# Attention feeding two MoE layers on one core: an earlier narrow transpose, pair 6 through the DRAM scratch, and a later sum of output halves

## The chip, the cores and the metric

One core of a Trainium2 chip runs the whole program in one launch. The metric is the device time in microseconds (us). The engines are called PE (TensorE, matmuls and transposes), DVE (VectorE), ACT (ScalarE), POOL (GpSimd) and SP (SyncE, which here only issues DMAs). Each works through its own queue in order.

## The reference

```python
# 2 x 8 heads, 768 rows, head size 64; bucketed attention
q_bits = einsum(q, proj) > 0; k_bits = einsum(k, proj) > 0      # 6 bits give a bucket
scores = q @ k.T / 8, and -1e9 where the buckets differ
attn = exp(scores - max); attn /= sum(attn) + 1e-9
x = attn @ v                                                     # to 1536 x 512
x = relu(x @ w_in)**2 @ w_out                                    # first MoE
x = silu(x @ w_in2) @ w_out2                                     # second MoE
```

Everything is float32.

## The kernel before

The heads are worked through as 8 pairs. A pair has 4 units (two heads, two halves of 384 rows), a unit has 3 tiles of 128 rows by 768 keys. So there are 32 units and 96 tiles. One loop over steps d sends out all instructions of attention; step d computes the scores of one tile, the exp of the tile before it, and transposes two blocks of 384 columns of exp'd tiles of an earlier unit. With `tc.manual_schedule()` the order on each engine is the order in which the code calls it; waits between engines follow from the tiles that they share.

In a step PE does, in this order, six transposes of 128 x 128 into two banks of PSUM (`transp`, L1025; three banks in turn), the product with V for the two blocks of two steps ago (`av`, L1049 and L1050), and the scores (`score_mm`, L989, two buffers in turn). Each transposed block goes through two instructions to become a high part, cast by ACT (`t_hi`, L1030), and a low part, subtracted by DVE (`t_lo`, L1036). DVE takes the row maximum (L996) and two short instructions on it (L1000, L1001); ACT then does the exp with its row sums (`score_exp`, L1009). When a unit is done, ACT copies its output out of PSUM (`ob`, L1060) and SP sends its two halves to the tiles `ta` and `tb` of the pair (L1062).

Once in 12 steps, at d = 5, 17, ..., 77, a step is long: PE multiplies by the projection (`bits_mm`, L789, 12 matmuls), DVE compares the result in two halves (`bits_cmp`, L795) and SP copies the bits into the score operands of a pair (`place_bits`, L919), whose first scores are computed two steps later. In these steps, and in 92 and 93, DVE also does one or two instructions of the conversion of a weight from 64 to 32 bits (`w_exp` L958, `w_sign` L962, `w_low` L966).

When pair p is done (d0 = 12(p + 1)), its row sums, 12 columns of 128 rows, are inverted (L1071) and brought into the layout of the output. For pairs 0 to 5 this is done with a narrow transpose at step d0 + 5 (`row_turn`, L1077), which writes into columns 384 to 511 of the bank whose first 384 columns hold block g + 1 of the step; ACT copies it out (L1079); SP puts it into a DRAM scratch (`row_put`, L1083) and gets it back, repeated over 64 partitions, three steps later (`row_get`, L1088). The narrow transpose stands behind both casts of its step in the code. For pair 6, POOL spreads the sums (L1074), PE transposes them at step 93 (`rb_mm`, L1097, six transposes) and ACT copies them out (L1108). Pair 7, the last, uses the same spreading and six transposes after the last step (L1315). POOL adds the two halves of the output, `ta` += `tb`, at step d0 + 3 (`x_sum`, L1103), multiplies by the rows (`x_mul`, L1115) and splits the first operands of the MoE (`x_put`, L1124 and L1125). At steps 83 to 89 POOL adds blocks of the result for the MoE (`x_form`, L1130).

After attention the MoE's instructions follow, ordered by a planner with its own costs. The change does not touch them.

Of the kernel before, what the change touches and what calls it, by code (L numbers as in the profile page):

```python
# [11 lines left out]
F32 = mybir.dt.float32  # L12
# [5 lines left out]
ALU = mybir.AluOpType  # L18
# [3 lines left out]
B, H, S, D = 2, 8, 768, 64  # L22
NT, DM, FF = B * S, H * D, 2048
NB = 6
NPAIR = B * H // 2
NU = NPAIR * 4
QW = 384
# [672 lines left out]
def lsh_attention_moe_moe(ctx, tc, kd, qk, qf, fq, v, pc, wi1, wo1, wi2, wo2, out):  # L700
# [109 lines left out]
    def first_load(h):  # L810
        t = pair[0]
        if h == 0:
            c = ac.tile([128, S], F32, tag="P", bufs=6, name="fc")
            first["c"] = c[:, 0:NFQ]
            first[0, 0] = c[:, NFQ : NFQ + QW], ac.tile([128, S], F32, tag="P", bufs=6, name="fq1")[:, 0:QW]
            k = a1.tile([128, S], F32, tag="ta", bufs=2, name="fk")
            first[0, 1] = k[:, half(0)], k[:, half(1)]
            nc.sync.dma_start(out=c[:, 0 : NFQ + QW], in_=fq)
            nc.scalar.dma_start(out=first[0, 1][0], in_=qf[0, 1, :, half(0)])
            nc.sync.dma_start(out=first[0, 1][1], in_=qf[0, 1, :, half(1)])  # L820
            nc.scalar.dma_start(out=first[0, 0][1], in_=qf[0, 0, :, half(1)])
        else:
            first[1, 0] = a1.tile([128, S], F32, tag="tb", name="fr10")
            first[1, 1] = a1.tile([128, 6, 2, 64], F32, tag="rw", bufs=2, name="fr11").rearrange("p a b c -> p (a b c)")
            for i in range(2):
                nc.sync.dma_start(out=first[1, i], in_=qf[1, i])
            nc.scalar.dma_start(out=pcr, in_=pc)
        t["qq"][h] = a1.tile([128, 2, S], F32R, tag="qq", bufs=2, name=f"qq0_{h}")
        t["kk"][h] = a1.tile([128, 2, S], F32R, tag="kk", bufs=2, name=f"kk0_{h}")
        if h == 0:  # L830
            first["hk", 0] = a1.tile([128, S], F32R, tag="hk", name="hk0_0")
# [209 lines left out]
    def av(g):  # L1041
        u, kt = divmod(g, KT)
        p, h, z = u // 4, (u // 2) % 2, u % 2
        if kt == 0:
            otile[u] = ps_o.tile([128, 512], F32, tag="o", name=f"o{u}") if u < NU - 1 else ps_s.tile([128, 2, 512], F32, tag="s", name=f"o{u}")[:, 0]
        o = otile[u]
        vv = pair[p]["vv"][:, h * KT + kt].rearrange("p a d -> p (a d)")
        th, tl = PT.pop(g)
        mm(o[:, 0:QW], vv, th, start=kt == 0, stop=False)  # L1049
        mm(o[:, 0:QW], vv, tl, start=False, stop=kt == KT - 1)  # L1050
        if kt == KT - 1:
            if p not in xs:
                xs[p] = [a1.tile([128, S], F32, tag=n, bufs=b, name=f"{n}{p}") for n, b in (("ta", 2), ("tb", 1))]
            if u == NU - 1:
                ta, zs = xs[p][0], slice(z * QW, (z + 1) * QW)
                nc.scalar.copy(out=ta[64:128, zs], in_=o[0:64, 0:QW])
                nc.vector.tensor_tensor(out=ta[64:128, zs], in0=o[64:128, 0:QW], in1=ta[64:128, zs], op=ALU.add)
                return
            ob = a2.tile([128, QW], F32, tag="ob", name=f"ob{u}")
            nc.scalar.copy(out=ob, in_=o[:, 0:QW])  # L1060
            for i in range(2):
                nc.sync.dma_start(out=xs[p][i][64 * h : 64 * h + 64, z * QW : (z + 1) * QW], in_=ob[64 * i : 64 * i + 64])  # L1062
# [6 lines left out]
    def norm_rows(p):  # L1069
        ri = sums[p]  # L1070
        nc.vector.reciprocal(out=ri, in_=ri)  # L1071
        if p >= NPAIR - 2:
            w = rows[p] = a1.tile([128, 6, 2, 64], F32, tag="rw", bufs=2, name=f"rw{p}")
            nc.gpsimd.tensor_copy(out=w, in_=ri.rearrange("p (h c) -> p c h", h=2).unsqueeze(3).broadcast_to([128, 6, 2, 64]))  # L1074

    def row_turn(p, t):
        nc.tensor.transpose(t[0:12, QW:512], sums[p], ident)  # L1077
        r = turned[p] = a1.tile([12, 128], F32, tag="rt", name=f"rt{p}")
        nc.scalar.copy(out=r, in_=t[0:12, QW:512])  # L1079

# [2 lines left out]
        nc.sync.dma_start(out=o.rearrange("h (c q) -> (h c) q", c=6), in_=turned[p])  # L1083

    def row_get(p):
        w = rows[p] = a1.tile([128, 6, 2, 64], F32, tag="rw", bufs=2, name=f"rw{p}")
        for h in range(2):
            nc.sync.dma_start(out=w[64 * h : 64 * h + 64].rearrange("p c h d -> p (c h d)"), in_=scratch[p][h : h + 1].broadcast_to([64, S]))  # L1088

    turned, scratch = {}, {}  # L1090
    rows = {}

    def rb_mm(p):
        s = ps_s.tile([128, 2, 512], F32, tag="s", name=f"rb{p}")
        for c in range(6):
            o = s[:, c // 3, c % 3 * 128 : c % 3 * 128 + 128]
            nc.tensor.transpose(o, rows[p][:, c].rearrange("p h d -> p (h d)"), ident)  # L1097
        return s

    def x_sum(p):  # L1100
        ta, tb = xs[p]
        for r, z in ((slice(0, 64), slice(QW, S)), (slice(0, 128), slice(0, QW))) if p == NPAIR - 1 else ((slice(0, 128), slice(0, S)),):
            nc.gpsimd.tensor_tensor(out=ta[r, z], in0=ta[r, z], in1=tb[r, z], op=ALU.add)  # L1103

    def x_norm(s, p):
        ta = xs[p][0].rearrange("p (a b) -> p a b", a=2)
        if p < NPAIR - 1:
            nc.scalar.copy(out=rows[p].rearrange("p c h d -> p (c h d)").rearrange("p (a b) -> p a b", a=2), in_=s[:, :, 0:QW])  # L1108
        else:
            nc.vector.tensor_tensor(out=x_rows(p).rearrange("p (a b) -> p a b", a=2), in0=s[:, :, 0:QW], in1=ta, op=ALU.mult)  # L1110

    def x_mul(p):
        if p < NPAIR - 1:
# [3 lines left out]
    def x_rows(p):  # L1117
        return yf[:, p % 4, p // 4 * S : p // 4 * S + S]
# [11 lines left out]
        nc.gpsimd.tensor_tensor(out=o, in0=o, in1=b, op=ALU.subtract if MINUS[0].get(k) else ALU.add)  # L1130

    todo = defaultdict(list)
    extra = defaultdict(list)
    mid = defaultdict(list)
    long, scale, turn = {}, {}, {}
    last = defaultdict(list)
# [1 line left out]
    def at(g, fn, *a):  # L1138
        todo[g].append((fn, a))
# [21 lines left out]
    for p in range(NPAIR):  # L1161
        d0 = 12 * (p + 1)
        at(d0 + (-3 if p < NPAIR - 1 else -4), norm_sums, p)
        at(d0 + (2 if p < NPAIR - 1 else -3), norm_rows, p)
        at(d0 + (3 if p < NPAIR - 1 else 0), x_sum, p)
        if p == NPAIR - 2:
            extra[d0 + 9].append((rb_mm, x_norm, p))
            at(d0 + 10, x_mul, p)
            at(d0 + 10, x_put, p)
        elif p < NPAIR - 2:  # L1170
            k = d0 + 5
            turn[k] = p
            at(k, row_put, p)
            at(k + 3, row_get, p)
            at(k + 5, x_mul, p)
            at(k + 5, x_put, p)

    for k, d in enumerate(X_STEPS):
        at(d, x_form, k)
# [14 lines left out]
    with tc.manual_schedule():  # L1194
# [63 lines left out]
        for d in range(-5, G // 2 + 3):  # L1258
            ready, new = new, None
            g = 2 * d  # L1260
            if ready:
                m = row_max(*ready)
            if 0 <= g - 1 < G and g - 1 not in early_lo:
                t_lo(g - 1)
            if ready:
                row_live(m)
            for fn, a in mid.pop(d, []):
                fn(*a)
            if 0 <= g < G and d in (92, 94):
                t = ps_s.tile([128, 2, 512], F32, tag="s", name=f"t{g}")  # L1270
                for i in range(2):
                    transp(g + i, t[:, i])
                t_hi(g)
                t_hi(g + 1)
                t_lo(g)
            elif 0 <= g < G:
                transp(g)
                t_hi(g)
                t_lo(g)
                transp(g + 1)  # L1280
                t_hi(g + 1)
                if d in turn:
                    row_turn(turn[d], PT[g + 1][0])
            more = extra.pop(d, [])
            if ready and more and d not in long:
                score_exp(*ready, m)
            if d in long:
                score_exp(*ready, m)
                if d in scale:
                    scale_q(scale.pop(d))  # L1290
            for n in (g - V_LAG, g + 1 - V_LAG):
                if 0 <= n < G:
                    av(n)
            if d in long:
                t = bits_mm(long[d])
            held = [(dve, pe(p), p) for pe, dve, p in more]
            if d in long:
                bits_cmp(t, long[d], 0)
                t_lo(g + 1)
                bits_cmp(t, long[d], 1)  # L1300
            for dve, t, p in held:
                dve(t, p)
            if ready and not more and d not in long:
                score_exp(*ready, m)
            u, j = divmod(d + 5, 3)
            if u < NU:
                new = u, j, score_mm(u, j)
            for fn, a in todo.pop(d, []) + last.pop(d, []):
                fn(*a)
            warm_up(WARM.get(d, 0))  # L1310
# [5 lines left out]
            ta = xs[p][0][:, z * QW : (z + 1) * QW]  # L1316
            nc.vector.tensor_tensor(out=x_rows(p)[:, z * QW : (z + 1) * QW], in0=t[:, 0:QW], in1=ta, op=ALU.mult)
        assert not new
        assert not todo and not extra and not mid and not scale
        att.close()  # L1320


# [62 lines left out]
```

## Time and profile before

| | us |
|---|---|
| timed runs, median of 3 | 729.46 (729.27 to 729.68) |
| the profiled execution | 728.33 |
| its span, first to last instruction | 726.6 |
| PE busy in the span | 714.7 |
| DVE busy | 610.8 |
| ACT busy | 539.7 |
| POOL busy | 258.7 |

The granted clock of PE is full (2.4 GHz) over the whole span. Attention takes the first 235 us or so, the MoE layers the rest. "Busy" is the time in which an engine had at least one instruction in work; instructions of an engine overlap at their ends, so the distance between two starts is shorter than a duration.

### The profile page before, as it was taken

How to read it: one execution, taken by the hardware profiler on the slowest of the kernel's cores; microseconds unless marked ns; L12 is line 12 of the kernel's file. 1: busy time of each engine (PE TensorE's matmuls, PEld its weight loads, DVE VectorE, ACT ScalarE, POOL GpSimd, SP SyncE). 2: the span in 40 equal slices, each digit the busy share in tenths (PEclk: the TensorE clock that was granted, in tenths of full speed). 3: DMA queues.
4: the chain of work that ended last, by engine and by line, in shares of the span. 5: the costliest groups of instructions: out<-in, count | busy, mean ns of one | idle time of the engine just before them, and what ended most of it. 6: DMA issues, size and time to landing. Idle time of an engine off the chain costs nothing.

```text
span 726.6 us, 10910 instructions
## 1 busy us (share of the span) xinstructions
PE 714.7 (98%) x3643; PEld 612.2 (84%) x3643; DVE 610.8 (84%) x1106; ACT 539.7 (74%) x1012; POOL 258.7 (36%) x242
## 2 busy tenths in 40 slices
PE   8999999999999999999999999999999999999998
PEld 4999898898899888888888888888788888888886
DVE  7999999999998979786797879989778778888840
ACT  6998898898798898486459568878766945854861
POOL 7634755656547512041231223234203110212300
PEclk9999999999999999999999999999999999999999
DMA  5887698697662536124534653368231332345432
GB/s 172 202 199 169 158 204 187 153 222 175 147 157 55 122 107 169 59 73 102 130 88 116 133 134 96 87 143 172 70 124 58 88 89 80 107 102 116 102 110 93
DMA packets 38640, 92.16 MB, mean 127 GB/s; under 512 B 5564, under 2 KB 10524, under 8 KB 38584
## 3 DMA queue, kind: packets, MB, share of 16 engines
q1 hardware_dynamic: 26120, 67.18, 31.7%
q0 software_dynamic: 12032, 23.79, 18.3%
q8 instruction: 29, 0.48, 0.3%
q10 hardware_dynamic: 432, 0.49, 0.2%
q14 instruction: 27, 0.22, 0.1%
HBM read 51.96 MB, written 3.18 MB: 76 GB/s over the span
## 4 chain that ended last, share of the span: by engine, by line
PE 80%; DVE 15%; ACT 3%; issue 1%; DMA 0%; POOL 0%; ACTq 0%; DVEq 0%; POOLq 0%
PE bank L558 36%; PE bank L443 24%; DVE mt L996 7%; PE bank L420 7%; DVE tl L1036 6%; PE s L989 3%; PE t L1025 3%; PE o L1049 2%; PE o L1050 2%; ACT P L1009 2%; PE bs L789 1%; PE bt L789 1%; DVE mt L1001 1%; ACT th L1030 1%; DVE mt L1000 1%
## 5 line engine op out<-in xcount | busy, mean ns | idle before, releaser
L558 PE MATMUL bank<-woh,cell 128*128 128x512 f32 (+1 forms) x392 | 120.0, 385 | 0.0
L558 PE MATMUL bank<-cell,woh 128*128 128x512 f32 x384 | 118.3, 389 | 0.0
L1036 DVE TENSOR_TENSOR tl<-t,th 128x384 fp32r<-128x384 f32 x192 | 104.7, 548 | 0.8 <-ACT th L1030 0.8
L1009 ACT ACTIVATE P<-s,mt 128x768 f32<-128x768 f32 x96 | 95.3, 993 | 11.2 <-DVE mt L1001 8.1
L996 DVE TENSOR_REDUCE mt<-s 128x1 f32<-128x768 f32 x96 | 91.5, 953 | 3.5 <-PE s L989 3.1
L1030 ACT CAST th<-t 128x384 fp32r<-128x384 f32 x192 | 81.9, 483 | 12.5 <-PE t L1025 12.1
L558 PEld LDWEIGHTS bank<-woh,cell 128*128 128x128 f32 x392 | 73.1, 188 | 14.7
L558 PEld LDWEIGHTS bank<-cell,woh 128*128 128x128 f32 x384 | 72.1, 188 | 15.2
L989 PE MATMUL s<-kk,qq 76*128 76x384 f32 (+1 forms) x384 | 83.8, 339 | 0.5 <-ACT P L1009 0.4
L1025 PE MATMUL t<-ident,P 128*128 128x128 f32 x576 | 78.9, 272 | 0.0
L278 DVE TENSOR_TENSOR cell<-bank,cell 128x512 f32<-128x512 f32 x91 | 62.1, 692 | 18.3 <-PE bank L443 13.9
L443 PE MATMUL bank<-xw,wpb 128*128 128x512 f32 x312 | 75.9, 389 | 0.0
L558 PE MATMUL bank<-wol,cell 128*128 128x512 f32 (+1 forms) x196 | 75.4, 385 | 0.0
L558 PE MATMUL bank<-cell,wol 128*128 128x512 f32 x192 | 74.7, 389 | 0.0
L1049 PE MATMUL o<-th,vv 128*128 128x384 f32 x192 | 72.5, 377 | 0.0
L1025 PEld LDWEIGHTS t<-ident,P 128*128 128x128 f32 x576 | 67.8, 140 | 4.5 <-DVE tl L1036 0.2
L989 PEld LDWEIGHTS s<-kk,qq 76*128 76x128 f32 (+1 forms) x384 | 68.3, 188 | 2.6 <-ACT P L1009 1.6
L443 PEld LDWEIGHTS bank<-xw,wpb 128*128 128x128 f32 x312 | 58.5, 188 | 12.4 <-DVE bank L278 0.3
L1050 PE MATMUL o<-tl,vv 128*128 128x384 f32 x192 | 64.3, 335 | 0.0
L588 ACT COPY yf<-bank 128x512 f32<-128x512 f32 x48 | 27.9, 586 | 35.4 <-PE bank L558 34.7
L450 ACT COPY cell<-bank 128x512 f32<-128x512 f32 x39 | 22.9, 587 | 40.7 <-PE bank L443 38.7
L268 ACT CAST cell<-cell 128x512 fp32r<-128x512 f32 x81 | 48.8, 617 | 1.9 <-DMA cell<-cell 0.8
(201 smaller groups left out, 1484.8 us busy)
## 6 DMA issues: line engine op xcount, KB each, us to landing
raw<-in_dram SPq DMA_DIRECT2D x64, 512.0 KB
cell<-cell POOLq DMA_DIRECT2D x23, 256.0 KB, 3.4
qq<-hq SPq DMA_DIRECT2D x28, 192.0 KB
kk<-in_dram POOLq DMA_DIRECT2D x14, 384.0 KB, 5.3
yf<-cell POOLq DMA_DIRECT2D x21, 256.0 KB, 3.3
vr<-in_dram SPq DMA_DIRECT2D x8, 384.0 KB
ta<-ob SPq DMA_DIRECT2D x31, 96.0 KB
tb<-ob SPq DMA_DIRECT2D x31, 96.0 KB
```

Of the source, the lines that this page charges most:

```text
L278: add("DVE", 0.70, lambda: vec.tensor_tensor(out=val(out), in0=bank[b], in1=val(other), op=ALU.add), [("bank", b), *reads], writes)
L420: mm(bank[b], wpa[n][:, p, 4 * h + j], x[:, q], start=j == 0 and z == 0, stop=j == 3 and z == 2)
L443: mm(bank[b], w[:, p], x[:, q], start=not started and z == 0, stop=z == 2, skip_group_check=started)
L558: mm(bank[b][:, 0:wd], x, y, start=start and i == 0 and z == 0, stop=i == (FB if half is None else 2 * half + 2) - 1 and z == 2, skip_grou ...
L989: mm(s[:, n, 0:QW], t["qq"][h][0:kk, ab, c0 : c0 + 128], t["kk"][h][0:kk, ab, n * QW : (n + 1) * QW], start=ab == 0, stop=ab == 1)
L996: nc.vector.tensor_reduce(out=m[:, 0:1], in_=s[:, :, 0:QW], op=ALU.max, axis=AX.XY, negate=True)
L1009: nc.scalar.activation(out=e.rearrange("p (a b) -> p a b", a=2), in_=s[:, :, 0:QW], func=AF.Exp, scale=m[:, 1:2], bias=m[:, 2:3], accum_ou ...
L1025: nc.tensor.transpose(t[:, j * 128 : (j + 1) * 128], P[u, j][:, kt * 128 : (kt + 1) * 128], ident)
L1030: nc.scalar.copy(out=th, in_=PT[g][0][:, 0:QW])
L1036: nc.vector.tensor_tensor(out=tl, in0=t[:, 0:QW], in1=th.bitcast(F32), op=ALU.subtract)
L1049: mm(o[:, 0:QW], vv, th, start=kt == 0, stop=False)
L1050: mm(o[:, 0:QW], vv, tl, start=False, stop=kt == KT - 1)
```

## The change

There are four edits.

- The narrow transpose is called right after the transposes of block g + 1 and before that block's cast; the copy of its result stays behind the cast (`row_turn` becomes `row_copy`).
- Pair 6 takes the way through the scratch too: narrow transpose and put at step 88, get at 90, multiplication at 93. `rb_mm`, the part of `x_norm` that is left and the list `extra` go away.
- `x_sum` moves from d0 + 3 to d0 + 6. `x_mul` of pairs 0 to 4 moves from d0 + 10 to d0 + 13 and `x_put` to d0 + 14; pair 5 keeps its steps.
- `tb` has two buffers instead of one, and the rows' tile `rw` one instead of two. Both are 128 x 768 float32.

```diff
-            first[1, 0] = a1.tile([128, S], F32, tag="tb", name="fr10")
-            first[1, 1] = a1.tile([128, 6, 2, 64], F32, tag="rw", bufs=2, name="fr11").rearrange("p a b c -> p (a b c)")
+            first[1, 0] = a1.tile([128, S], F32, tag="tb", bufs=2, name="fr10")
+            first[1, 1] = a1.tile([128, 6, 2, 64], F32, tag="rw", name="fr11").rearrange("p a b c -> p (a b c)")
...
-                xs[p] = [a1.tile([128, S], F32, tag=n, bufs=b, name=f"{n}{p}") for n, b in (("ta", 2), ("tb", 1))]
+                xs[p] = [a1.tile([128, S], F32, tag=n, bufs=b, name=f"{n}{p}") for n, b in (("ta", 2), ("tb", 2))]
...
     def norm_rows(p):
         ri = sums[p]
         nc.vector.reciprocal(out=ri, in_=ri)
-        if p >= NPAIR - 2:
-            w = rows[p] = a1.tile([128, 6, 2, 64], F32, tag="rw", bufs=2, name=f"rw{p}")
+        if p == NPAIR - 1:
+            w = rows[p] = a1.tile([128, 6, 2, 64], F32, tag="rw", name=f"rw{p}")
             nc.gpsimd.tensor_copy(out=w, in_=ri.rearrange("p (h c) -> p c h", h=2).unsqueeze(3).broadcast_to([128, 6, 2, 64]))
 
-    def row_turn(p, t):
-        nc.tensor.transpose(t[0:12, QW:512], sums[p], ident)
+    def row_copy(p, t):
         r = turned[p] = a1.tile([12, 128], F32, tag="rt", name=f"rt{p}")
         nc.scalar.copy(out=r, in_=t[0:12, QW:512])
...
-        at(d0 + (3 if p < NPAIR - 1 else 0), x_sum, p)
-        if p == NPAIR - 2:
-            extra[d0 + 9].append((rb_mm, x_norm, p))
-            at(d0 + 10, x_mul, p)
-            at(d0 + 10, x_put, p)
-        elif p < NPAIR - 2:
-            k = d0 + 5
+        at(d0 + (6 if p < NPAIR - 1 else 0), x_sum, p)
+        if p < NPAIR - 1:
+            k = d0 + (5 if p < NPAIR - 2 else 4)
             turn[k] = p
             at(k, row_put, p)
-            at(k + 3, row_get, p)
-            at(k + 5, x_mul, p)
-            at(k + 5, x_put, p)
+            at(k + (3 if p < NPAIR - 2 else 2), row_get, p)
+            x = k + (8 if p < NPAIR - 3 else 5)
+            at(x, x_mul, p)
+            at(x + 1 if p < NPAIR - 3 else x, x_put, p)
...
                 t_lo(g)
                 transp(g + 1)
+                if d in turn:
+                    nc.tensor.transpose(PT[g + 1][0][0:12, QW:512], sums[turn[d]], ident)
                 t_hi(g + 1)
                 if d in turn:
-                    row_turn(turn[d], PT[g + 1][0])
+                    row_copy(turn[d], PT[g + 1][0])
```

## Rows read from the trace of the kernel before

**Rows 1.** Stages of the span: length, then busy us (instructions) of each engine.

```profile
core 0: us, PE busy (x) PEld busy (x) DVE busy (x) ACT busy (x) POOL busy (x), PEclk, DMA share, GB/s
54.50:195.10 140.60, 135.43 (x907) 128.43 (x907) 134.82 (x324) 123.81 (x273) 85.33 (x75) 1.00 0.75 175
```

**Rows 2.** Waits of PE, whole span: who waited for whom, us, times, longest.

```profile
PE t L1077 <- ACT th L1030: 6.2, 6, 1.0
```

**Rows 3.** Order of time, step 29: start, duration, engine, line, output<-inputs [idle before].

```profile
80.74 0.82 PE L1025 MATMUL t<-ident,P 128*128 128x128 f32 x6
82.60 0.27 PE L1077 MATMUL t<-ident,sums 128*12 128x128 f32 x1 [1.04 <-ACT th L1030]
86.21 0.82 PE L1025 MATMUL t<-ident,P 128*128 128x128 f32 x6
...
81.60 0.86 ACT L1030 CAST th<-t 128x384 fp32r<-128x384 f32 x2
```

**Rows 4.** Order of time on PE: transposes of steps 5 and 6.

```profile
25.86 0.82 PE L1025 MATMUL t<-ident,P 128*128 128x128 f32 x6
...
30.02 0.82 PE L1025 MATMUL t<-ident,P 128*128 128x128 f32 x6
```

**Rows 5.** The chain that ended last, step 93: start, us, what.

```profile
229.83 0.66 PE rb L1097 x6
```

**Rows 6.** Order of time on DVE: first compare of steps 17, 29 and 41.

```profile
56.56 0.67 DVE L795 TENSOR_SCALAR bt<-bs,tmt 48x384 fp32r<-48x384 f32 x1 [0.58 <-PE bs L789]
...
84.66 0.67 DVE L795 TENSOR_SCALAR bt<-bs,tmt 48x384 fp32r<-48x384 f32 x1 [0.71 <-PE bs L789]
...
112.75 0.67 DVE L795 TENSOR_SCALAR bt<-bs,tmt 48x384 fp32r<-48x384 f32 x1 [1.04 <-PE bs L789]
```

**Rows 7.** Order of time, step 77: POOL's sum and DVE's weight instruction.

```profile
194.20 1.84 POOL L1103 TENSOR_TENSOR ta<-ta,tb 128x768 f32<-128x768 f32 x1
...
194.90 1.70 DVE L966 SCALAR_TENSOR_TENSOR both<-raw,both 128x512 uint32<-128x512 uint32 x1
```

**Rows 8.** Order of time: bits DMAs, score matmuls two steps on, and one landing.

```profile
59.15 1.06 SPq L919 DMA_DIRECT2D kk<-bt  x1
61.54 0.87 PE L989 MATMUL s<-kk,qq 128*128 128x384 f32 x4
...
87.27 0.76 SPq L919 DMA_DIRECT2D kk<-bt  x1
89.64 0.86 PE L989 MATMUL s<-kk,qq 128*128 128x384 f32 x4
...
171.55 1.08 SPq L919 DMA_DIRECT2D kk<-bt  x1
173.93 0.91 PE L989 MATMUL s<-kk,qq 128*128 128x384 f32 x4
...
233.05 0.60 SPq L1062 DMA_DIRECT2D tb<-ob  x1
235.28 1.02 POOL L1103 TENSOR_TENSOR ta<-ta,tb 128x384 f32<-128x384 f32 x1 [0.19 <-DMA tb<-ob]
```

**Rows 9.** Order of time, steps 92 to the end of attention.

```profile
228.49 0.30 POOL L1067 TENSOR_SCALAR sums<-sums 128x8 f32<-128x8 f32 x1 [1.28 <-ACT P L1009]
...
230.13 0.68 DVE L966 SCALAR_TENSOR_TENSOR both<-raw,both 128x512 uint32<-128x512 uint32 x1
...
232.17 1.95 DVE L1036 TENSOR_TENSOR tl<-t,th 128x384 fp32r<-128x384 f32 x4 [0.34 <-ACT th L1030]
...
234.50 0.82 PE L1315 MATMUL rb<-ident,rw 128*128 128x128 f32 x6
```

**Rows 10.** Order of time: pair 5's put, get and use; step 88's first ob DMA.

```profile
197.21 0.40 SPq L1083 DMA_DIRECT2D rows<-rt  x1
208.48 1.16 SPq L1088 DMA_DIRECT2D rw<-rows  x2
...
221.33 0.46 SPq L1062 DMA_DIRECT2D ta<-ob  x1
...
213.33 1.84 POOL L1115 TENSOR_TENSOR yf<-rw,ta 128x768 f32<-128x768 f32 x1 [8.36 <-DMA rw<-rows]
```

More of the change, by code (lines that the diff above doesn't have):

```diff
@@ L1085, in row_get @@
     def row_get(p):
-        w = rows[p] = a1.tile([128, 6, 2, 64], F32, tag="rw", bufs=2, name=f"rw{p}")
+        w = rows[p] = a1.tile([128, 6, 2, 64], F32, tag="rw", name=f"rw{p}")
         for h in range(2):
@@ L1091, in lsh_attention_moe_moe @@
     rows = {}
[L1093 to L1098, printed above, removed]
     def x_sum(p):
@@ L1103, in x_sum @@
             nc.gpsimd.tensor_tensor(out=ta[r, z], in0=ta[r, z], in1=tb[r, z], op=ALU.add)
[L1105 to L1110, printed above, removed]
     def x_mul(p):
@@ L1132, in lsh_attention_moe_moe @@
     todo = defaultdict(list)
-    extra = defaultdict(list)
     mid = defaultdict(list)
@@ L1280, in lsh_attention_moe_moe @@
                 transp(g + 1)
+                if d in turn:
+                    nc.tensor.transpose(PT[g + 1][0][0:12, QW:512], sums[turn[d]], ident)
                 t_hi(g + 1)
                 if d in turn:
-                    row_turn(turn[d], PT[g + 1][0])
-            more = extra.pop(d, [])
-            if ready and more and d not in long:
-                score_exp(*ready, m)
+                    row_copy(turn[d], PT[g + 1][0])
             if d in long:
@@ L1295, in lsh_attention_moe_moe @@
                 t = bits_mm(long[d])
-            held = [(dve, pe(p), p) for pe, dve, p in more]
             if d in long:
@@ L1300, in lsh_attention_moe_moe @@
                 bits_cmp(t, long[d], 1)
-            for dve, t, p in held:
-                dve(t, p)
-            if ready and not more and d not in long:
+            if ready and d not in long:
                 score_exp(*ready, m)
@@ L1318, in lsh_attention_moe_moe @@
         assert not new
-        assert not todo and not extra and not mid and not scale
+        assert not todo and not mid and not scale
         att.close()
```

## The prediction

> **What bounds the kernel now.** I read the table by stage first. Where attention has its narrow transposes, TensorE (PE) is busy 135.43 of 140.60 us, VectorE (DVE) 134.82, ScalarE (ACT) 123.81 [rows 1]. Next, the waits: PE's longest line in the whole execution is six waits of the narrow transpose L1077 for ACT's cast L1030, 6.2 us together [rows 2], and the list has no PE line of the MoE part. So whatever attention gains or loses on PE reaches the end, if DVE can follow. The third view is the order of work in one such step: PE starts its transposes at 80.74, the narrow one only at 82.60, the next step's transposes at 86.21, 5.47 us in all [rows 3]. The one step that has the same bits matmuls but no narrow transpose runs from 25.86 to 30.02, 4.16 us [rows 4].
>
> **Part 1: the narrow transpose ahead of the cast.** In the chain six transposes of 128 columns hold 0.66 us [rows 5], so the narrow one, of 128 columns too, costs 0.11. Without its wait a turn step should last 4.16 + 0.11 = 4.27 us where it lasts 5.47: 1.20 each. The six read 5.44 to 5.47, 32.78 together, so 7.16 in all; more than the 6.2 of the wait, since the pipe also drains and fills.
> The wait changes sides: the second cast of the step now comes behind the narrow transpose in the same bank. That one would start near 81.4 and, with its 0.27, end by 81.7; the second cast is the later half of the two that run from 81.60 to 82.46 [rows 3] and starts near 82.0. Hidden, by 0.3 us; if that cover were gone, the cast, the copy of the sums and the exp behind them on ACT would move by the difference, and two steps on the score matmul.
> The Trainium skill ("PSUM — Partial Sum Buffer", PSUM bank collisions raise a hardware error) wants any two engines kept apart per bank and quadrant, even on other columns. By that rule the cast can't be spared this wait; the trace shows its mirror image, the 1.04 at 82.60.
>
> **What is late next: DVE.** In a turn step DVE waits for the bits matmuls before its compare L795: 0.58 at 56.56, 0.71 at 84.66 (the step at 140.86 is like it), 1.04 at 112.75 [rows 6]. With the bits 1.20 earlier this idle time is used up, and 0.08 by which DVE instructions overlap; DVE then falls behind PE by the rest: 0.54, 0.41 twice, 0.08. In the last two turn steps a weight instruction runs long beside POOL's x_sum, 1.70 for L966 [rows 7] against 0.68 [rows 9]; x_sum leaves for the next step, so I count 0.08 and 0.2 there. Sum: 1.7 us.
> Does this lateness stop PE? The step behind a turn step has one DVE subtraction less (0.55), so the buffers recover. But the bits go by DMA (L919, which waits for the compare in SP's queue) to the score matmul two steps on. A DMA lands about 1.63 after its issue ends: tb<-ob is issued from 233.05 to 233.65 and POOL, waiting for it, starts at 235.28 [rows 8]. For the bits this means 60.21 + 1.63 = 61.84 for a pass that starts 0.35 after 61.54, 0.05 to spare; 88.03 + 1.63 = 89.66 against 89.99, 0.33 to spare; and 172.63 + 1.63 = 174.26 against 174.28, where the four matmuls are already stretched, 0.91 for 0.86 [rows 8]. With DVE's lateness taken off these margins about 0.5 is lost at 61.5, 0.1 each at 89.6, near 146, at 174 and near 202: 0.9. The issue of 1.06 at 59.15 is long beside the 0.76 at 87.27; with the shorter one 0.3 of it goes. I take **0.7**, ends 0 (the landing is not that tight) and 1.7 (all of DVE's lateness stops PE).
>
> **Part 2: pair 6 through the scratch.** Added at step 88: one narrow transpose, 0.11 on a PE without gaps, and one 0.25 copy on ACT, which idles 16.8 of 140.60 us [rows 1] and makes it up within a few steps. Off POOL: a copy of 0.82. Off PE at step 93: six transposes, 0.66 [rows 5]; off ACT there: a copy of 0.80. So 0.66 is the most that can come. But DVE's last subtractions L1036 end at 232.17 + 1.95 = 234.12, and PE has only its last product left before L1315 at 234.50 [rows 9]. Ahead of them DVE waited 0.34 for casts; beyond that it sets the pace, so about 0.4 can be had.
> Against it: x_mul of pair 6 on POOL (1.84) moves to just behind norm_sums, which ends at 228.79 [rows 9], if the rows are there. The ob DMAs of step 88 start at 221.33 [rows 10]; with the added copy's 0.25 ahead of them and their 0.46 and 0.6, the put goes near 222.7 and lands some 2.0 later, the get goes at 224.8 to 225.9 and lands near 228.3 (an estimate: 1.63 after the issue, and most of a microsecond for twice 192 KB). Then POOL works from 228.9 to 230.75, and DVE's L966 at 230.13 [rows 9] meets it. When the same instruction began while POOL ran to 196.04, it ended 0.56 after POOL [rows 7]. So it would end near 231.3 instead of 230.8, and the six subtractions behind it are 0.5 late. What is left of the 0.4 the narrow transpose of step 88 takes: **0.0**, ends 0.6 gain (L966 goes first) and 0.8 loss (POOL starts just ahead of it).
> [...]
>
> **Part 3: the sum at step 6, tb in two buffers.** x_sum moves back three steps, x_mul and x_put of pairs 0 to 4 three and four. All are POOL's, which today sits idle before x_mul for the row DMA (8.36 for pair 5 [rows 10]); with that time spent on other work, the kk loads and casts behind it come earlier. SP's tb DMA no longer waits for x_sum. PE waits for none of these today [rows 2], so I count 0. If POOL were late, next in its queue are the kk load of the second head, needed six steps later, and the split for the bits, needed ten steps later. One rw buffer less costs nothing: each get comes seven steps after the multiplication that frees it.
>
> **Sum.** 7.16 - 0.7 - 0.0 = 6.4 us, rounded. The profiled execution took 728.33 (span 726.6 and 1.7 around it), so it would become 721.9; the median of the timed runs is 1.13 higher, 729.46, which gives **723.1**. Bounds: 7.16 + 0.6 = 7.8 and 7.16 - 1.7 - 0.8 = 4.7.
>
> **Rivals.**
> *All of it comes* (chance 0.20): DMAs land sooner than 1.63 after issue, or L966 goes first. 7.2 to 7.8 us, about 722.0. For it: most bits DMAs make their step today with no visible stop. Against it: 173.93, where the stretch is there already [rows 8].
> *DVE becomes the bound* (0.14): its 134.82 of 140.60 us [rows 1] are nearly all that PE leaves after the change (140.60 less some 6). The lateness is carried on, and the end loses 0.8: 4.7 us, 724.8. Against it: the subtraction less behind each turn step.
> *The wait stays* (0.05): the narrow transpose is held by something that the cast hides today. Then only the end of attention is left, 729.0 to 729.6.
> *Pair 6's rows come late* (0.04), the slower side. POOL works in order: behind x_mul wait the copy for pair 7's rows, behind that PE's L1315 and all of the MoE. For pair 5 the trip from put to use took 197.21 to 213.33, 16.1 us [rows 10]. The same from 222.7 ends at 238.8; x_mul's 1.84 and the copy's 0.82 make it 241.5, where PE after its gains would want L1315 at 234.50 - 0.55, 7.5 us sooner. The gains are 6.46 and 0.55, so the kernel is 0.5 slower, 729.9, and 731 with a trip of 17.2. It decides from a landing near 231.3 on. Against it: of the 16.1, 11.3 were the queue ahead of the get at 208.48 [rows 10], and between steps 88 and 90 SP has nothing else.
>
> **Chances.** The forecast (722.4 to 723.9 by itself) has 0.57. The range 721.6 to 725.0 takes in the first two rivals and 0.2 for the scatter of timed runs. A measurement of this kernel can tell about 0.2%, 1.5 us. Faster by more: 0.57 + 0.20 + 0.14 = 0.91; within: 0.05; slower: 0.04.
>
> **What will show it.** Right, if L1077 is gone from the waits, turn steps last near 4.3 us, the compare no longer waits for the bits in steps with two weight instructions, and short waits for the bits' DMA appear at the score matmul two steps on. At the end L966 should last 1 us or more beside x_mul. Wrong, if PE waits for DVE or ACT in every turn step (DVE is the bound), or if L1315 waits for POOL (the rows came late).

## The result, and the profile after

The changed kernel takes 723.5 us (median; 723.25 to 723.72), the kernel before 729.4 us beside it: ratio 0.992, interval 0.9903 to 0.9937. The prediction was 723.1 us, faster. Its profiled execution took 723.25, with a span of 721.5 instead of 726.6 us.

First the waits of PE in the changed kernel, whole span (who waited for whom, us, times, longest):

```profile
PE warm L980 <- DVE zero L1183: 1.3, 1, 1.3
PE bank L420 <- DVE ta L1057: 0.6, 1, 0.6
...
PE t L1025 <- DVE tl L1036: 0.3, 1, 0.3
```

The six waits of the narrow transpose [rows 2] are gone. Two lines are new, both at the end of attention: L420, the MoE's first matmul, waits for DVE, and the transposes L1025 of step 95 wait 0.3 for a subtraction.

Then the order of time in step 29 of the changed kernel, the same step as in [rows 3]: start, duration, engine, line, output<-inputs. A step is counted from its first transpose L1025 to that of the next step; a turn step is one of the six with a narrow transpose (17, 29, ..., 77).

```profile
80.32 0.82 PE L1025 MATMUL t<-ident,P 128*128 128x128 f32 x6
80.98 0.27 PE L1263 MATMUL t<-ident,sums 128*12 128x128 f32 x1
84.59 0.82 PE L1025 MATMUL t<-ident,P 128*128 128x128 f32 x6
...
81.18 0.86 ACT L1030 CAST th<-t 128x384 fp32r<-128x384 f32 x2
...
83.44 0.66 DVE L795 TENSOR_SCALAR bt<-bs,tmt 48x384 fp32r<-48x384 f32 x1
...
86.04 0.77 SPq L919 DMA_DIRECT2D kk<-bt  x1
...
85.95 0.88 PE L989 MATMUL s<-kk,qq 128*128 128x384 f32 x4
88.02 1.01 PE L989 MATMUL s<-kk,qq 128*128 128x384 f32 x4
```

The narrow transpose starts 0.66 behind the six, without a wait, and the step lasts 84.59 - 80.32 = 4.27 us instead of 5.47. The two casts still take 0.86 together. The compare shows no idle time before it (0.71 in [rows 6]). And two steps on, the score matmuls at 88.02 are stretched, 1.01 for 0.88. The later two of the four, the second pass, read the bits; the issue for kk ends at 86.81, and by that stretch the second pass, due at 88.02 + 0.35, starts at about 88.50, 1.7 behind it.

Last, the end of attention, order of time in the changed kernel:

```profile
222.66 0.29 POOL L1067 TENSOR_SCALAR sums<-sums 128x8 f32<-128x8 f32 x1 [2.21 <-ACT P L1009]
223.03 1.84 POOL L1100 TENSOR_TENSOR yf<-rw,ta 128x768 f32<-128x768 f32 x1
224.30 1.12 DVE L966 SCALAR_TENSOR_TENSOR both<-raw,both 128x512 uint32<-128x512 uint32 x1
228.63 0.82 PE L1292 MATMUL rb<-ident,rw 128*128 128x128 f32 x6
229.38 0.56 DVE L1057 TENSOR_TENSOR ta<-o,ta 64x384 f32<-64x384 f32 x1 [1.09 <-ACT ta L1056]
230.00 1.19 PE L420 MATMUL bank<-xk,wpa 128*128 128x512 f32 x4 [0.56 <-DVE ta L1057]
```

POOL multiplies pair 6 right behind norm_sums, so its rows were there. L966 takes 1.12 us beside it, and ends at 225.42, 0.55 behind POOL; the wait of 0.3 at step 95 follows from that (the last run below, in which L966 goes first, has no such wait). The last six transposes come at 228.63 (234.50 in [rows 9]). The MoE's first matmul follows 1.37 us later. In the kernel before it followed after 0.57 us:

```profile
235.07 3.21 PE L420 MATMUL bank<-xk,wpa 128*128 128x512 f32 x13
235.20 0.56 DVE L1057 TENSOR_TENSOR ta<-o,ta 64x384 f32<-64x384 f32 x1 [1.08 <-ACT ta L1056]
```

There L420 did not wait for L1057.

The sum, between the two profiled executions:

| | us |
|---|---|
| six turn steps, 5.47 to 4.27 | -7.16 |
| stretched steps 19, 31, 55, 79 (2.30, 2.20, 2.24, 2.19 for 2.055) | +0.71 |
| narrow transpose of pair 6 in step 88 | +0.11 |
| step 91 to the last six transposes, 9.10 to 9.07 | -0.03 |
| from these to the MoE's first matmul, 0.57 to 1.37 | +0.80 |
| start of the program (step 5 at 26.39 instead of 25.86) | +0.53 |
| sum | -5.04 (span: -5.1) |

The start is not the change's: in a second execution of the same kernel step 17 begins at 52.60, where the kernel before has 52.64.

### The profile page after: what moved, and what is told of

Same layout as the page of the kernel before. It is cut to its first block, busy times and chain, and to the rows that moved or that the text cites. A ratio compares the mean times of both kernels' runs of the same rounds, so it can differ in the third digit from the quotient of the medians.

```text
span 721.5 us, 10904 instructions
## 1 busy us (share of the span) xinstructions
PE 715.2 (99%) x3637; PEld 612.0 (85%) x3638; DVE 609.2 (84%) x1106; ACT 538.7 (75%) x1012; POOL 256.9 (36%) x241
## 4 chain that ended last, share of the span: by engine, by line
PE 98%; DVE 1%; ACT 0%; issue 0%; ACTq 0%; DVEq 0%
PE bank L558 36%; PE bank L443 24%; PE s L989 9%; PE t L1025 9%; PE bank L420 7%; PE o L1049 5%; PE o L1050 5%; PE bs L789 1%; PE bt L789 1%; PE warm L980 1%; DVE mt L996 0%; ACT P L1009 0%; PE bs L900 0%; PE bf L884 0%; PE t L1263 0%
## 5 line engine op out<-in xcount | busy, mean ns | idle before, releaser
L1036 DVE TENSOR_TENSOR tl<-t,th 128x384 fp32r<-128x384 f32 x192 | 104.7, 548 | 0.5 <-ACT th L1030 0.5
L1025 PE MATMUL t<-ident,P 128*128 128x128 f32 x576 | 79.2, 273 | 0.3 <-DVE tl L1036 0.3
L1025 PEld LDWEIGHTS t<-ident,P 128*128 128x128 f32 x576 | 68.0, 140 | 5.1 <-DVE tl L1036 0.7
```

What stands on the lines that cost most here:

```text
L1025: nc.tensor.transpose(t[:, j * 128 : (j + 1) * 128], P[u, j][:, kt * 128 : (kt + 1) * 128], ident)
L1036: nc.vector.tensor_tensor(out=tl, in0=t[:, 0:QW], in1=th.bitcast(F32), op=ALU.subtract)
```

## The experiments

The theory: the gain is the wait of the narrow transpose, and DVE's lateness gives part of it back through the bits' DMA. Rivals: the later sum and the second buffer bring part of it, or are needed for it. All times below are medians beside the kernel before on the same chip (728.9 for the first four runs, 729.4 for the next four, 729.3 for the last ones). Differences of under about 1 us between variants of the changed kernel are not clear of the scatter of their runs; there the traces are compared step by step.

### The narrow transpose alone

```diff
+                if d in turn:
+                    nc.tensor.transpose(PT[g + 1][0][0:12, QW:512], sums[turn[d]], ident)
                 t_hi(g + 1)
                 if d in turn:
-                    row_turn(turn[d], PT[g + 1][0])
+                    row_copy(turn[d], PT[g + 1][0])
```

> The kernel before with the first edit alone: the narrow transpose of pairs 0 to 5 ahead of the second cast; pair 6 keeps its way through POOL and PE, the sum keeps its step, the buffers are as before. If the whole gain is the wait of the narrow transpose: turn steps 4.27 us instead of 5.47, 7.16 us less, and 0.7 to 1.0 us given back at the score matmul two steps on (the sum of halves still collides with DVE's weight instruction, so DVE is a little later than in the changed kernel). The six transposes at step 93 and the last unit's output keep their banks, so the MoE's first matmul L420 follows the last transposes by 0.57 us as before, without a wait for L1057. Time 722.8 to 723.4. Rival: the gain needs the other edits too (pair 6, later sum): 726 or more.

Measured: 726.8 us (724.6 to 731.2), ratio 0.997 (0.9957 to 0.9986). Neither theory nor rival is right as put: a third of the gain comes, with more scatter than in any other run. The turn steps last 4.27 as expected, but in the profiled execution (724.6) the two steps behind each give back 3.5 us, where the changed kernel loses 0.7. That execution is one of the two fastest of twelve; what the median one loses beyond it, 2.2 us, stands in no trace. Order of time of this kernel, steps 41 to 44:

```profile
108.99 1.86 POOL L1102 TENSOR_TENSOR ta<-ta,tb 128x768 f32<-128x768 f32 x1
109.38 2.03 DVE L962 SCALAR_TENSOR_TENSOR wi<-raw,wi 128x512 uint32<-128x512 uint32 x1
111.93 0.55 PE L1025 MATMUL t<-ident,P 128*128 128x128 f32 x3
113.07 0.52 PE L1025 MATMUL t<-ident,P 128*128 128x128 f32 x3 [0.59 <-DVE tl L1036]
116.28 1.08 PE L989 MATMUL s<-kk,qq 128*128 128x384 f32 x4
```

DVE's weight instruction L962 meets POOL's sum and lasts 2.03 us instead of 0.68. DVE is then so late that PE's transposes wait for a subtraction (0.59 at 113.07), and the bits stretch the score pass at 116.28. In this trace four weight instructions are hit (1.30, 2.03, 1.33, 0.86 us). The kernel before has such meetings too, 1.08 us at 166.78 and 1.70 at 194.90 [rows 7], but there DVE's idle time before the compare covered them: at 168.95, behind the first, 0.63 of it was left, and behind the second none, with no stop of PE.

### The other edits alone

```diff
-                if d in turn:
-                    nc.tensor.transpose(PT[g + 1][0][0:12, QW:512], sums[turn[d]], ident)
                 t_hi(g + 1)
                 if d in turn:
+                    nc.tensor.transpose(PT[g + 1][0][0:12, QW:512], sums[turn[d]], ident)
                     row_copy(turn[d], PT[g + 1][0])
```

> The changed kernel with the narrow transpose put back behind the second cast: the other edits alone. If the gain is the wait alone: seven waits of about 1.04 us on PE, each with its step about 1.2 us longer; against the kernel before one turn step more (+1.2, for pair 6), about 0.6 less at step 93, and about +0.8 for the MoE's first matmul, which waits for L1057; so 730.2 to 731.0, slower than before by 0.8 to 1.6. Rival: the later sum and the second buffer bring part of the gain: under 729.

Measured: 731.1 us, ratio 1.003 (1.0019 to 1.0042). As the theory has it: seven waits of the narrow transpose, 7.1 us in all, and L420's wait of 0.55. By themselves the other edits cost time.

### The order of the MoE's banks, in the changed kernel and in the kernel before

```diff
-    idle = [2, 3, 4, 7, 0, 1, 5, 6]
+    idle = [0, 1, 4, 7, 2, 3, 5, 6]
```

In the changed kernel:

> The changed kernel with another order of the PSUM banks that the MoE takes first: 0, 1, 4, 7, 2, 3, 5, 6 instead of 2, 3, 4, 7, 0, 1, 5, 6. Nothing of attention changes. Theory: without the six transposes of pair 6 the score buffers alternate one time fewer, so the last unit's output lies in banks 2 and 3, and the MoE's first matmul L420, which takes bank 2, waits for DVE to read it (L1057). With bank 0 first the wait of 0.56 us goes, L420 follows the last transposes by 0.57 us instead of 1.37: 0.8 us less than the changed kernel, about 722.7. Rival: L420 waits for something else, such as the operands: 723.5, the wait stays under another name.

In the kernel before:

> The kernel before with the bank order of the run above, and nothing else. Theory: before, the last unit's output lies in banks 0 and 1, so with bank 0 first the MoE's first matmul has to wait for L1057 as it does in the changed kernel: 0.8 us more than before, about 730.2. Rival (the bank has nothing to do with it): 729.4, no such wait.

Measured: 723.3 us (0.992; 0.9904 to 0.993) and 729.9 us (1.001; 1.0003 to 1.002). The traces are plain. First the changed kernel with the new order, then the kernel before with it:

```profile
229.22 0.81 PE L1292 MATMUL rb<-ident,rw 128*128 128x128 f32 x6
229.79 1.39 PE L420 MATMUL bank<-xk,wpa 128*128 128x512 f32 x5
```

```profile
235.31 0.82 PE L1315 MATMUL rb<-ident,rw 128*128 128x128 f32 x6
236.63 1.67 PE L420 MATMUL bank<-xk,wpa 128*128 128x512 f32 x6 [0.50 <-DVE ta L1057]
```

The wait goes from the one (0.57 behind the transposes) and comes to the other (1.32). So it is the bank: the score buffers alternate one time fewer without the six transposes of pair 6, and the last unit's output lies where the MoE begins. In the time it shows for the kernel before (+1.0) and not for the changed one, whose median is the same as without the edit. The 0.80 by which step 91 to L420 is shorter went elsewhere in that execution: beside the second execution of the changed kernel (next section) it started 0.6 later, its steps lost 0.1 more, and the MoE took 0.1 more. So the seam's 0.8 us is shown in the traces, and in the time of the changed kernel it is not.

### The changed kernel again

No edit.

> The changed kernel again, beside the runs below on one chip: 723.5 us. In its trace the step with the first stop at the bits (step 19) should scatter from run to run if that stop is a DMA's landing: 0.25 us in the first trace, 0.8 in the run with the other bank order, where nothing else of attention differs.

Measured: 723.3 us. Step 19 lasts 2.76, so 0.71 is lost there, not 0.25. Bits and score matmuls of this execution:

```profile
58.44 1.24 SPq L919 DMA_DIRECT2D kk<-bt  x1
60.33 0.51 PE L989 MATMUL s<-kk,qq 128*128 128x384 f32 x2
61.24 0.62 PE L989 MATMUL s<-kk,qq 76*128 76x384 f32 x2 [0.40 <-DVE tl L1036]
```

The second pass starts 1.56 behind the end of the issue, and the issue took 1.24 us, where it took 0.77 in the first execution. With the other bank order it took 1.35, and 0.82 was lost. Two other runs fit between: an issue of 0.92 with 0.39 lost (the last run below) and one of 0.99 with 0.44 (the narrow transpose alone). (The profile puts the wait down to L1036, which had ended before; what came last is the DMA.)

### One weight instruction out of four of the turn steps

```diff
-W_STEPS = ((0, 5, 17, 17, 29), (8, 17, 29, 41, 53), (30, 41, 53, 65, 77), (54, 65, 77, 92, 93))
+W_STEPS = ((0, 5, 17, 18, 29), (8, 17, 30, 41, 53), (30, 41, 54, 65, 77), (54, 65, 78, 92, 93))
```

> The changed kernel with one of the two weight instructions that DVE does in each of the steps 17, 29, 53 and 77 moved to the step behind; same work. Theory: DVE's lateness in the turn steps is what makes the bits late; with 0.42 to 0.68 us less of DVE work ahead of the compares, the bits are placed sooner by about that, and the stops of PE at the score matmul two steps on shrink from 0.25, 0.14, 0.18 and 0.14 us to nothing at steps 19, 31, 55 and 79: 0.6 to 0.7 less than the changed kernel, 722.8. Step 67, where one weight instruction stays, has none today. Rival (the compare waits for the bits matmuls anyway, or the stop is not the bits'): 723.5.

Measured: 724.2 us (723.6 to 724.7), by the median 0.9 slower than the changed kernel beside it (723.1 to 724.4); this is not clear of the scatter, but the expected gain did not come. Steps 30 and 31 of this run:

```profile
85.22 1.29 POOL L974 TENSOR_TENSOR wpa<-wi,wpa 128x512 fp32r<-128x512 f32 x1
85.44 0.77 SPq L919 DMA_DIRECT2D kk<-bt  x1
85.70 1.10 DVE L958 TENSOR_SCALAR wi<-wi 128x512 uint32<-128x512 uint32 x1
...
86.48 2.00 POOL L1095 TENSOR_TENSOR ta<-ta,tb 128x768 f32<-128x768 f32 x1
87.32 0.55 PE L1025 MATMUL t<-ident,P 128*128 128x128 f32 x3 [0.44 <-DVE tl L1036]
88.40 0.86 PE L989 MATMUL s<-kk,qq 128*128 128x384 f32 x4
```

The mechanism holds: the pass at 88.40 is no longer stretched, and step 79 lasts 2.05, without a stop. The time does not follow. In the step behind, DVE has no idle time for the instruction either. It makes the subtraction late that frees a buffer for PE's transposes (0.44 at 87.32), and at steps 30 and 54 it meets POOL's split of the weight, L974, which runs from 85.22 to 86.52: 1.10 us instead of 0.42. The sum, which starts at 86.48 while L958 still runs, takes 2.00 instead of 1.84. Steps 31 and 55 lose 0.65 each. Steps 19 and 67 lose 0.24 and 0.30 to the bits, the latter with an issue of 1.26.

### The sum at its old step

```diff
-        at(d0 + (6 if p < NPAIR - 1 else 0), x_sum, p)
+        at(d0 + (3 if p < NPAIR - 1 else 0), x_sum, p)
```

> The changed kernel with the sum of output halves back at step d0 + 3; its second operand keeps two buffers. Theory A (collision): the sum then runs beside DVE's weight instruction in several turn steps, as in the run with the narrow transpose alone (1.30, 2.03, 1.33 and 0.86 us instead of 0.68); with no wait of PE left that covers it, DVE's lateness stops PE in the two steps behind, in all 2 to 3 us more than in the changed kernel: 725.5 to 726.5, with scatter. Theory B (the second buffer brings the gain, since SP's queue, with the bits in it, no longer waits for the sum): 723.5, no stops of transposes for DVE.

Measured: 723.7 us (0.992; 0.9908 to 0.9935), 0.4 above the changed kernel, within the scatter. Theory A falls as it was put: the sum at its old step meets one weight instruction only (1.07 us at 162.84). POOL in this run, and below it POOL with the narrow transpose alone:

```profile
72.92 1.83 POOL L1100 TENSOR_TENSOR yf<-rw,ta 128x768 f32<-128x768 f32 x1
77.32 1.83 POOL L1095 TENSOR_TENSOR ta<-ta,tb 128x768 f32<-128x768 f32 x1 [0.54 <-DMA tb<-ob]
```

```profile
74.26 1.85 POOL L1114 TENSOR_TENSOR yf<-rw,ta 128x768 f32<-128x768 f32 x1 [8.15 <-DMA rw<-rows]
80.59 1.86 POOL L1102 TENSOR_TENSOR ta<-ta,tb 128x768 f32<-128x768 f32 x1
```

With the narrow transpose alone POOL stands 8.15 us before x_mul for the rows, and everything behind, the sum included, is late and falls into the turn step. With x_mul moved, the sum is done before it. So by these traces it is not the sum's step that matters, but the multiplication's; the next run but one tries that alone.

### One buffer for tb

```diff
-                xs[p] = [a1.tile([128, S], F32, tag=n, bufs=b, name=f"{n}{p}") for n, b in (("ta", 2), ("tb", 2))]
+                xs[p] = [a1.tile([128, S], F32, tag=n, bufs=b, name=f"{n}{p}") for n, b in (("ta", 2), ("tb", 1))]
```

> The changed kernel with one buffer for the second operand (tb) instead of two; the sum stays at d0 + 6. Theory B: SP's issue of the next pair's tb waits for the sum, which ends about 4 us behind the turn step's start plus 4; the bits' two issues stand behind it in SP's queue and go 3 to 4 us later, so PE stops by 2.5 to 3.5 us two steps on, in up to six places: 738 to 743. Rival (the second buffer only saves a wait that nobody waits for): 723.5.

Measured: 771.1 us, ratio 1.057 (1.056 to 1.0589): theory B's mechanism with about three times its price. POOL's sum, SP's queue and the score matmuls:

```profile
59.81 1.82 POOL L1095 TENSOR_TENSOR ta<-ta,tb 128x768 f32<-128x768 f32 x1
...
61.66 0.46 SPq L1062 DMA_DIRECT2D tb<-ob  x1
...
64.16 0.76 SPq L919 DMA_DIRECT2D kk<-bt  x1
...
61.01 0.51 PE L989 MATMUL s<-kk,qq 128*128 128x384 f32 x2
68.86 1.01 PE L989 MATMUL s<-kk,qq 76*128 76x384 f32 x2 [7.34 <-DMA kk<-bt]
```

SP issues tb only when the sum has ended (61.63), the bits go behind it, and they land 3.9 us after the issue instead of 1.6. Then a second price, from the table by stage (length, busy us of PE, PEld, DVE, ACT, POOL, granted clock, DMA share, GB/s):

```profile
62.00:69.00 7.00, 0.14 (x1) 0.14 (x1) 0.00 (x0) 0.67 (x2) 2.72 (x3) 0.72 0.96 212
69.00:72.00 3.00, 3.00 (x12) 2.90 (x13) 2.07 (x5) 1.25 (x3) 2.77 (x4) 0.50 1.06 229
72.00:75.00 3.00, 3.00 (x13) 2.90 (x12) 1.26 (x2) 1.18 (x3) 2.07 (x2) 0.50 0.80 204
```

While PE stands for these 7.3 us its granted clock falls (a mean of 0.72 from 62 to 69), it is half (1.2 GHz) from 69 to 75 us, and the steps behind last 3.84 and 2.94 instead of 2.06. At the first place 8.0 + 1.8 + 0.9 = 10.7 us are lost, at five places 48 together.

### The narrow transpose and the later multiplication

The kernel before with the edit of the first run, and this one (the sum at d0 + 3, one tb, pair 6 as before):

```diff
-            at(k + 5, x_mul, p)
-            at(k + 5, x_put, p)
+            x = k + (8 if p < NPAIR - 3 else 5)
+            at(x, x_mul, p)
+            at(x + 1 if p < NPAIR - 3 else x, x_put, p)
```

> The kernel before with the narrow transpose ahead of the second cast and x_mul and x_put of pairs 0 to 4 three and four steps later, as in the changed kernel; the sum stays at d0 + 3, tb keeps one buffer, pair 6 its way through POOL and PE. Theory: in the run with the narrow transpose alone POOL came late to the sum, because x_mul, waiting for its rows, stood ahead of it (74.26 after 8.15 us of waiting; the sum at 80.59, beside DVE's weight instruction); with x_mul behind, the sum runs at about 77.3 as in the run with the early sum and two buffers, and the collisions and stops are gone but for one near step 66: about 1 us of stops instead of 4, the MoE's first matmul follows at 0.57, step 93 keeps its six transposes: 723.0 to 723.8, less scatter. Rival (it is the second buffer of tb that does it): 726 to 727 as with the narrow transpose alone.

Measured: 723.1 us (722.6 to 724.2), ratio 0.992 (0.9905 to 0.9933), span 721.1. The theory holds. One weight instruction is hit (0.93 us at 109.11) instead of four, and the stops are 1.6 us instead of 3.5 (0.7 of it at step 19, with an issue of 1.21, and 0.4 at step 67). L420 follows the last transposes by 0.57, and step 91 to L420 takes 9.70 us, before 9.68, in the changed kernel 10.44. As far as the scatter can tell, these two edits have the whole gain of the four.

### The bits for kk issued by ACT, and then two more edits

```diff
-            nc.sync.dma_start(
+            (nc.scalar if (n, h) == (1, 0) else nc.sync).dma_start(
```

> The changed kernel with one DMA in each long step issued by ACT instead of SP: the bits of the first head for kk (L919). Today it stands behind the issue of qq's bits, which takes 0.80 us. Theory: the stops at steps 19, 31, 55 and 79 (0.25, 0.15, 0.18, 0.14 us, in another run 0.71 at the first) are kk's landing; issued 0.8 earlier it lands in time and they go: 0.6 to 0.7 less than the changed kernel, 722.8, the pass no longer stretched (0.86). Cost: ACT's queue holds the issue and waits for DVE's compare, near 111.85, while ACT idles from 111.6 to 112.2; if the issue holds ACT for 0.8, casts come up to 0.5 later, and some of it may reach PE. Rival (kk is not what the pass waits for): 723.5, stops as before.

Measured: 724.0 us (723.4 to 724.3), about 0.6 above the changed kernel, again not clear of the scatter and without the expected gain. Steps 30 and 31:

```profile
85.42 0.81 SPq L919 DMA_DIRECT2D qq<-bt  x1
85.42 0.76 ACTq L919 DMA_DIRECT2D kk<-bt  x1
86.28 0.86 ACT L1030 CAST th<-t 128x384 fp32r<-128x384 f32 x2 [2.06 <-DVE mt L996]
86.90 1.05 PE L1025 MATMUL t<-ident,P 128*128 128x128 f32 x6
88.49 0.86 PE L989 MATMUL s<-kk,qq 128*128 128x384 f32 x4
```

Again the landing is in time (0.86 at 88.49), and again PE stops elsewhere: ACT stands behind its issue, which waits for the compare and lasts until 86.18; the casts come late (86.28), and the transposes are stretched (1.05 for 0.82). Steps 7, 19, 31, 55 and 79 lose 0.71, 0.34, 0.24, 0.2 and 0.25.

With the other bank order and L966 at step 92:

```diff
-    idle = [2, 3, 4, 7, 0, 1, 5, 6]
+    idle = [0, 1, 4, 7, 2, 3, 5, 6]
...
-W_STEPS = ((0, 5, 17, 17, 29), (8, 17, 29, 41, 53), (30, 41, 53, 65, 77), (54, 65, 77, 92, 93))
+W_STEPS = ((0, 5, 17, 17, 29), (8, 17, 29, 41, 53), (30, 41, 53, 65, 77), (54, 65, 77, 92, 92))
```

> The run above plus the other order of the MoE's banks, plus DVE's last weight instruction (L966) one step earlier, at 92, so that it runs ahead of POOL's multiplication of pair 6. Theory: 0.6 to 0.7 from the bits, 0.8 from L420's wait for L1057, and up to 0.4 from L966 at 0.68 instead of 1.12 us: 721.5 to 722.0. Rival: the end of attention is set by DVE's subtractions whatever their start, and L420 then waits for operands of the MoE: 722.3 to 722.8.

Measured: 722.7 us, ratio 0.991. Step 91 to L420 takes 8.96 us, 1.5 less than in the changed kernel; ACT's issue eats a good part of it. So these two without ACT's issue:

> The changed kernel with the other order of the MoE's banks and DVE's last weight instruction (L966) at step 92; all bits are issued by SP again. In the run with all three, step 91 to the MoE's first matmul took 8.96 us (10.44 in the changed kernel), but ACT's issue of a DMA cost about 0.7 at step 7 and 0.9 in the steps 19 to 79, in place of the bits' stops of 0.7. Theory: without it the 1.48 us at the end of attention stay and the bits' stops return: 723.4 - 1.5 = 721.9. Rival (what is won at the end of attention is lost again in the MoE's start): 722.7.

Measured: 722.0 us (721.3 to 722.7), ratio 0.990 (0.987 to 0.9921), span 719.5: the best of all. The end of attention:

```profile
222.57 0.69 DVE L966 SCALAR_TENSOR_TENSOR both<-raw,both 128x512 uint32<-128x512 uint32 x1
222.68 2.29 POOL L1100 TENSOR_TENSOR yf<-rw,ta 128x768 f32<-128x768 f32 x1
227.61 0.82 PE L1292 MATMUL rb<-ident,rw 128*128 128x128 f32 x6
228.18 2.07 PE L420 MATMUL bank<-xk,wpa 128*128 128x512 f32 x8
```

L966 goes first and keeps its 0.69; POOL's multiplication pays, 2.29 for 1.84, and nobody waits for that.

## Why the prediction came out right

**Part 1** held to the digit: 4.27 us a turn step, 7.16 in all, the second cast hidden. The wait that the Trainium skill's rule on bank collisions ("PSUM — Partial Sum Buffer", PSUM bank collisions raise a hardware error) asks of the second cast cost nothing here: the narrow transpose ended at 81.25, and the two casts last 0.86 us, as before.

**DVE next.** Right in mechanism: the compare no longer waits, PE stops where the bits are read two steps on, and moving DVE's work or the bits' issue takes the stretch away at that place (though not the time). In size 0.7 was predicted, 0.7 and 1.2 were seen in two executions. The landing is 1.56 to 1.7 after the issue (1.63 predicted), but the issue at step 17 took 0.77 in one execution, 1.24 in the other, and that decides whether step 19 loses 0.25 or 0.71. Why the same issue takes longer in some executions was not found.

**Part 2** held in both its halves. L966 took 1.12 us beside x_mul, the rows were there at 223.03, step 91 to the last transposes was the same within 0.03. The gain's end, L966 first, was worth 0.67 from step 91 to the last transposes (8.40 for 9.07). The put landed sooner than forecast: its issue ended at 217.18 and the get started at 218.38, 1.2 later, not 2.0; this was on no path.

**What failed: the seam to the MoE.** The prediction read from PE's waits that the MoE part has none, and so that whatever attention gains reaches the end. It costed rb_mm by its 0.66 on PE and by its copy, and did not count that it also takes a turn of the score buffers. With one turn less, L420 waits for L1057: 0.8 us in the traces, moved both ways by the bank order.

**Part 3: right by its zero, wrong by its reason.** "PE waits for none of these today" is true of the kernel before, where DVE's idle time before the compare (0.58 to 1.04 [rows 6]) covered POOL's meetings with DVE. Part 1 removes that cover. Beside the kernel before, the narrow transpose alone brings 2.1 us and with the later multiplication 6.2, so some 4 us of the gain do not come without it. The two traces show 2.0 of these as stops (3.5 against 1.6, the first from one of the fastest executions of its run). The prediction let the sum leave the turn step and put nothing against it; the run with the sum at its old step shows that it leaves because x_mul no longer stands ahead of it. The second tb is worth 48 us with the sum at its new step (771.1 against 723.5), but the sum's move brings 0.4 at most, and with both left out the time is the same (723.1). What the prediction lacked among its rivals is an edit off the critical path that the main edit needs.

So 6.4 us were forecast, and 5.1 came between the two profiles (5.6 without the later start); the 1.3 that lack are the seam's 0.8 and the start's 0.5. The forecast put the median 1.13 above the profiled execution, as in the kernel before (728.33 to 729.46), and in the changed kernel it stands only 0.25 above (723.25 to 723.50). These 0.9 hide most of what the sum lacked, and the time came out 0.4 above the forecast. That it came so near is in this part luck: the mechanism of parts 1 and 2 and of DVE's lateness was right, the seam was missed.

## What to carry to other kernels

When an edit takes away a wait, list what the wait was covering, on every engine, and price it without the cover: here DVE's idle time hid meetings with POOL, and some 4 us of the gain did not come once it was gone, and what fixed them was to take a long wait (x_mul for its rows) out of the head of an in-order queue. When an instruction is removed, count the buffers that it took in turn as well as its time: with two buffers in turn, an odd or even number of uses decides who stands in whose bank where the next stage begins. Where PE, DVE and ACT were all nearly full, two tries to move a late piece of work away (a weight instruction by a step, a DMA issue to ACT) only moved the stop.

## What the runs showed of the hardware

- A weight instruction with both inputs in SBUF and an operation of POOL that was already running: 0.68 us became 0.86 to 2.03, and it ended 0.54 to 0.56 behind POOL's each time. With DVE first POOL took 2.29 for 1.84. L958, with one input, in SBUF, took 1.10 for 0.42 us beside POOL's L974. The Trainium skill ("SBUF — State Buffer", Who interferes with whom) names both cases: DVE instructions in the two-port modes beside those with two SBUF inputs. The trace agrees with the page in that both met POOL; in which mode L958 ran, no trace shows.
- The same small DMA landed 1.56 to 1.7 us after its issue where a pass waited for it. It took 3.9 us in a stretch with 212 GB/s of DMA traffic; whether that traffic is the cause, no run shows.
- A DMA issued by ACT held ACT for the whole issue: 0.76 us (ACT's next cast began 0.10 behind its end), and 1.63 in the step behind step 5.
- A stop of 7.3 us on PE, in which the granted clock fell, was followed by some 6 us at half of it (0.50), 2.7 us more on top of the stop.
